# FFN2 of two batches as seven block products, four softmax products on another engine, and a new order of pieces

## The chip, the cores and the metric

The kernel runs on one core of a Trainium2 chip. The metric is the device time of one execution in microseconds, as the median of several runs. The core has five engines, each of which works through its own queue in order: TensorE (PE, matmuls into PSUM), VectorE (DVE), ScalarE (ACT), GpSimd (POOL) and SyncE (SP, which here only issues DMAs). PSUM is one tile of eight banks, each 128 partitions by 512 float32. DMAs are issued by POOL (loads that cast float32 to bfloat16, and phi), SP and ACT (stores).

## The reference

The input is q, k, v with 8 batches, 8 heads, 576 positions and 64 columns, phi with 32 memory slots, and four weights. Attention goes through the slots, and a feed-forward network with a maximum of three products follows:

```python
a = exp(phi - max_s(phi)); a = a / sum_s(a)                 # over the 576 positions
k_m = einsum('bhsm,bhsd->bhmd', a, k)                       # 32 slots a head
v_m = einsum('bhsm,bhsd->bhmd', a, v)
attn = softmax(q @ k_m^T / 8)                               # over the 32 slots
x = (attn @ v_m), heads side by side                        # 4608 rows, 512 columns
h = maximum(maximum(x @ w1, x @ w2), x @ w3)                # 768 columns
out = h @ w_out                                             # 4608 rows, 512 columns
```

## The kernel before, in words

The work is cut into pieces. The string of words at lines 594 to 617 is the order in which they are issued: a word like `F6@1!` is piece F with index 6 of batch 1, and the mark `!` swaps the engine that empties PSUM (`EVAC`, line 164, gives the usual one: a for ACT, v for DVE). Each engine gets its instructions in this order, so the order of words is the order within every engine and every queue. A second string (lines 138 to 146) says which PSUM bank each piece takes; a piece that takes a bank waits until the piece that had it before has been emptied. Nothing else schedules the work.

The pieces, by letter:

- L and H load: `L0@b` is phi, `L1@b` k, `L2@b` v, `L3@b` q of batch b (lines 85 to 112), all but the first phi issued by POOL. A load is put behind whatever POOL has been given before it. k and v have two buffers (`kvo`), so have phi and q. Y loads the weights.
- E (line 229) takes the exponential of phi on ACT. r (line 103) packs k (`r0`) or v (`r1`) on POOL into `kvr`, beside a column of ones.
- B (line 249) multiplies the exponentials with k, v and the ones: 72 small matmuls. N (lines 269 to 290) normalises on DVE, K (line 298) transposes the result on PE.
- Q (line 313) transposes q on DVE, in two halves. S (line 333) makes the scores of a batch from them on PE, and ACT takes two exponentials (line 342).
- a, s, c, m, X (lines 387 to 417) are the softmax over the 32 slots, per half g of the heads: DVE transposes in blocks of 32, sums, takes the reciprocal, POOL multiplies (m, line 409), DVE transposes back into `attn`.
- D (line 440) folds the values into the weights: `D0` to `D2` give `wp` for w1 - w3 and w2 - w3, `D3` gives `wp3` for the part of w3 that goes straight to the output (w3 times w_out, made once). Batch 0 has other columns.
- F (line 466) is the first layer: twelve per batch, four matmuls of 288 columns each. An even one is emptied through a relu into `h`, an odd one goes through a maximum on DVE with the `h` before it into `hT` (line 479).
- T (lines 497 and 506) is FFN2 for 128 rows: six matmuls of `hT` with w_out and two of `attn` with `wp3`, 512 columns each, then a copy to `ot` and a store of 256 KB by SP. Two batches have 1152 rows, nine tiles; `T4` is the tile that spans both. The last tile of all is done in two halves (lines 538 and 546).
- W, O, V prepare weights at the start; Z, I, M, R belong to the start as well.

The part of this order that the prediction follows is where batches 2 to 4 overlap (lines 601 to 607) and where B, S and the packs of each batch stand.

Of the kernel before, what the change touches and what calls it, by code (L numbers as in the profile page):

```python
# [8 lines left out]
FP32 = mybir.dt.float32  # L9
BF16 = mybir.dt.bfloat16  # L10
# [5 lines left out]
def kernel(  # L16
# [33 lines left out]
    opool = ctx.enter_context(tc.tile_pool(name="opool", bufs=6))  # L50
# [34 lines left out]
    def load_ph(b):  # L85
        ph = inp.tile([P, NP, NC, M], FP32, name="ph")
        loaded.setdefault(b, {})["ph"] = ph
        dst = ph.rearrange("p j c m -> p j (c m)")
        if b == 0:
            for h in halves:  # L90
                nc.sync.dma_start(out=dst[:, h], in_=by_pair(phi, b)[:, h])
        else:
            nc.gpsimd.dma_start(out=dst, in_=by_pair(phi, b))

    def load_kv(b, i, h=slice(0, NP)):
        kv = loaded.setdefault(b, {})["kv"] = kvos[b % 2]
        nc.gpsimd.dma_start(  # L97
            out=kv[:, 1 - i, h].rearrange("p j c d -> p j (c d)"),
            in_=by_pair((k, v)[i], b)[:, h],
        )  # L100

    def pack(b, i):
        nc.gpsimd.tensor_copy(  # L103
            out=kvrs[b % 2][:, :, :, D * i : D * (i + 1)], in_=kvos[b % 2][:, 1 - i]
        )
# [125 lines left out]
    def k_and_ones(kv, r, j, c):  # L231

        flat = kv[r].rearrange("p i j c d -> p (i j c d)")
        k0 = (NP * NC + j * NC + c) * D
        step = 2 * NP * NC * D - k0
        return flat[:, k0 : k0 + 2 * step].rearrange("p (i x) -> p i x", i=2)[:, :, 0:D]

    def att_kv(b, part=None):
        s = st[b]
        kvp = two_banks()  # L240
        s["kvp", part] = kvp
        kv = loaded[b]["kv"]
        nd = {None: 2 * D + 1, 0: 2 * D, 1: D}[part]
        kvr = kvrs[b % 2]
        for c in range(NC):
            for j in range(NP):
                for a in range(NG):
                    r = slice(HP * a, HP * (a + 1))
                    nc.tensor.matmul(  # L249
                        kvp[M * j : M * (j + 1), a, 0:nd],  # L250
                        lhsT=s["e"][r, j, c, :],
                        rhs={
                            None: lambda: kvr[r, j, c, 0:nd],
                            0: lambda: k_and_ones(kv, r, j, c),
                            1: lambda: kv[r, 0, j, c, :],
                        }[part](),
                        start=(c == 0),
                        stop=(c == NC - 1),
                        tile_position=(HP * a, M * j),
                    )  # L260

    def att_kv_norm(b, part=None):
# [16 lines left out]
        if part == 1:  # L279
            return  # L280
        for g in range(NG):
# [3 lines left out]
                in0=kvp[:, g, 0:D]  # L285
# [77 lines left out]
    def ones_rec(b, g):  # L363
# [7 lines left out]
        r = work.tile([P, S], FP32, name="r")  # L371
# [84 lines left out]
    def ffn1(b, n, swap):  # L456
# [20 lines left out]
        else:  # L477
# [6 lines left out]
            )  # L484

# [75 lines left out]
    def issue(b, n, swap):  # L561
# [8 lines left out]
            "r": lambda: pack(b, i),  # L570
# [9 lines left out]
            "m": lambda: att_mul(b, i),  # L580
# [5 lines left out]
            "T": lambda: ffn2(b, i, swap),  # L586
            "W": lambda: w3_t(i, swap),
# [6 lines left out]
    for w in """  # L594
        E@0 H2@0 H0@0 L3@0 Z25@0 B0@0 Y2@0 I@0 N0@0 Z2@0 K0@0! Q0@0 Q1@0 Z9@0 S@0 Z2@0 M0@0 M1@0
        R0@0 R1@0 W0@0 Y3@0 W1@0 W2@0 Z6@0 O1@0 H3@0 O3@0 O2@0 H1@0 X1@0 B1@0 X0@0 N1@0
        K1@0 O0@0 Y0@0 D1@0! D0@0! D3@0 F8@0 F10@0 F2@0 V0@0 F6@0 F0@0! Y1@0 D2@0 D4@0 F4@0
        L0@1 V1@0 F1@0 E@1 F3@0 L1@1 F5@0 F9@0 F7@0 L3@1 F11@0 B0@1 T3@0 N0@1 K0@1! L2@1 Q1@1
        L2@2 L1@2 Q0@1 L0@2 V2@0 T0@0! L3@2 S@1 T1@0 a0@1 s0@1 c0@1 m0@1 B1@1 N1@1 a1@1 L1@3
        K1@1 s1@1 D0@1 D1@1! D2@1 c1@1 m1@1 X0@1 L3@3 r1@2 X1@1 T2@0! L2@3 F6@1 F10@1 F7@1 F2@1  # L600
        F3@1 F4@1 F0@1 r0@2 E@2 F5@1 F1@1 F11@1 L0@3 L0@4 F8@1 L2@4 F9@1 B@2 D3@1 N@2 Q1@2
        T0@1! K@2 T2@1! r0@3 Q0@2 S@2 a0@2 a1@2 s1@2 c1@2 m1@2 T4@1! D1@2! s0@2 D2@2 c0@2 m0@2
        X1@2 D0@2 T3@1 Q0@3 L3@4 X0@2 Q1@3 T1@1 F0@2 F4@2 F8@2 F6@2 F9@2 E@3 F7@2 r1@3 F5@2
        F10@2 F1@2 B@3 L1@4 D3@2 N@3 L0@5 F2@2 F11@2 E@4 F3@2 L1@5 K@3 r1@4 L2@5 T2@2! S@3 T3@2
        a0@3 s0@3 c0@3 m0@3 D0@3 D2@3 a1@3 s1@3 c1@3 X0@3 D1@3! Q0@4 m1@3 T1@2 L3@5 L2@6 T0@2!
        X1@3 F10@3 r0@4 F2@3 F4@3 E@5 Q1@4 r0@5 F5@3 F3@3 L1@6 F8@3 B@4 N@4 D3@3 F9@3 F6@3
        F11@3 L0@6 K@4 F0@3 F7@3 F1@3 S@4 a0@4 T4@3! s0@4 a1@4 D0@4 c0@4 s1@4 r1@5 c1@4 D3@4
        m0@4 X0@4 Q0@5 T0@3! D1@4! D2@4 B@5 T3@3 m1@4 X1@4 L0@7 F10@4 Q1@5 N@5 F8@4 K@5 F6@4
        F9@4 S@5 F7@4 L3@6 F2@4 F4@4 a0@5 L1@7 a1@5 F0@4 s0@5 r1@6 F3@4 D0@5 r0@6 s1@5 c1@5 E@6
        D3@5 m1@5 c0@5 F1@4 T1@3 L2@7 F11@4 L3@7 E@7 F5@4 m0@5 B@6 D1@5! D2@5 X1@5 N@6 T2@3!  # L610
        X0@5 F6@5 F8@5 Q0@6 Q1@6 K@6 F4@5 F9@5 S@6 F7@5 r0@7 a0@6 F2@5 a1@6 s0@6 c0@6 F0@5
        F10@5 m0@6 F1@5 s1@6 c1@6 F11@5 F5@5 T0@4! F3@5 X0@6 T2@4! r1@7 D0@6 D1@6! Q0@7 B@7
        m1@6 N@7 X1@6 T2@5! K@7 T3@4 Q1@7 S@7 a0@7 F2@6 s0@7 a1@7 s1@7 c1@7 m1@7 c0@7 F4@6
        T4@5! D3@6 D2@7 D0@7! T0@5! D3@7 D2@6 X1@7 m0@7 D1@7! T1@4 X0@7 F6@7 F3@6 T1@5 F4@7
        F8@7 F0@7 F5@6 F10@6 F7@7 F9@7 F10@7 F5@7 F0@6 F11@7 F6@6 F1@7 F7@6 F2@7 F8@6 F11@6
        F9@6 F1@6 F3@7 T0@6! T0@7! T3@5 T2@7! T2@6! T1@6 T1@7 T3@6 T4@7! T3@7
    """.split():
        n, b = w.rstrip("!").split("@")
        issue(int(b), n, w.endswith("!"))
# [30 lines left out]
```

## Time and profile before

| what | us |
|---|---|
| median of 3 runs | 164.94 |
| lowest, highest | 164.56, 165.78 |
| span of the profiled execution, first to last instruction | 163.3 |
| PE busy | 153.8 |
| ACT, DVE, POOL busy | 100.6, 90.4, 69.5 |

The profiled execution comes with its span and not with a time of its own; the median of the runs is 1.6 us above that span. The mean granted clock of TensorE was 0.995. The page gives for each group of instructions the line, engine, operation, tile, shapes, count, the busy time with the mean of one, and the idle time before it with what ended it. The chain follows the last instruction back to what released it, step by step. The DMA share of a window is the mean busy share of the 16 DMA engines; it can go above 1 where packets of two queues overlap.

### The profile page before, as it was taken

The page shows a single profiled execution, that of the slowest core. Times are in us where ns is not written, and L with a number is a line of the kernel's source. Part 1 is how long each engine was busy: PE and PEld are TensorE (multiplying, and loading weights), DVE is VectorE, ACT ScalarE, POOL GpSimd, SP SyncE. Part 2 cuts the span into 40 slices and gives each one's busy share as a digit, 9 for nine tenths or more (in the row PEclk, how much of TensorE's full clock was granted, in tenths as well). Part 3 has the DMA queues.
Part 4 walks back from the last instruction along what each step waited for, and adds up shares of the span by engine and source line. Part 5 has one row for each costly group of instructions (what it writes and reads, how often), then busy time and mean ns, then how long its engine had stood idle before and what let it go on. Part 6 is the DMA issues. An engine that isn't in the chain of part 4 may idle for free.

```text
span 163.3 us, 4838 instructions
## 1 busy us (share of the span) xinstructions
PE 153.8 (94%) x2080; PEld 85.3 (52%) x2080; DVE 90.4 (55%) x181; ACT 100.6 (62%) x151; POOL 69.5 (43%) x71
## 2 busy tenths in 40 slices
PE   7978798899899999999999999999999999999990
PEld 2433444564377436743673575576553468744450
DVE  2023704798838665849399748879749128810010
ACT  4205445845497488778885899994658976223320
POOL 7932205100599259657968957646403100000000
PEclk9999999999999999999999999999999999999998
DMA  6999999999999999999999999996313130014333
GB/s 150 152 206 207 205 210 217 274 208 210 253 313 238 209 253 379 274 210 293 252 263 206 232 355 264 191 233 150 130 69 129 69 128 0 0 68 186 135 128 130
DMA packets 21974, 31.77 MB, mean 195 GB/s; under 512 B 1216, under 2 KB 16576, under 8 KB 21952
## 3 DMA queue, kind: packets, MB, share of 16 engines
q0 software_dynamic: 16080, 21.43, 68.7%
q1 hardware_dynamic: 5728, 9.90, 17.2%
q8 instruction: 16, 0.26, 0.6%
q10 hardware_dynamic: 144, 0.13, 0.2%
q14 instruction: 6, 0.05, 0.1%
HBM read 39.32 MB, written 9.44 MB: 299 GB/s over the span
## 4 chain that ended last, share of the span: by engine, by line
PE 83%; DMA 9%; POOL 2%; ACT 2%; issue 1%; DVE 1%; ACTq 0%; POOLq 0%
PE psum L497 29%; PE psum L466 28%; DMA wo_sb<-in_moe_w_out_dram 9%; PE psum L506 8%; PE psum L440 6%; PE psum L249 4%; PE psum L192 3%; PE psum L333 2%; PE psum L515 1%; ACT h L170 1%; PE psum L538 1%; PE psum L298 1%; POOL kvo L97 1%; ACT wp L172 1%; POOL qq L110 0%
## 5 line engine op out<-in xcount | busy, mean ns | idle before, releaser
L497 PE MATMUL psum<-wo_sb,hT 128*128 128x512 bf16 x210 | 51.3, 380 | 0.0
L466 PE MATMUL psum<-attn,wp 128*128 128x288 bf16 x384 | 50.5, 286 | 0.1
L479 DVE TENSOR_TENSOR hT<-psum,h 128x576 bf16<-128x576 f32 x48 | 34.2, 749 | 18.0 <-PE psum L466 12.5
L466 PEld LDWEIGHTS <-wp 128*128 128x128 bf16 x384 | 36.7, 98 | 13.2 <-issue 2.0
L172 ACT COPY ot<-psum 128x512 f32<-128x512 f32 x35 | 20.7, 591 | 32.1 <-PE psum L506 25.2
L497 PEld LDWEIGHTS <-hT 128*128 128x128 bf16 x210 | 19.2, 97 | 24.0 <-issue 4.3
L172 ACT CAST wp<-psum 128x1024 bf16<-128x1024 f32 (+1 forms) x31 | 29.2, 995 | 3.8 <-PE psum L440 2.0
L103 POOL COPY kvr<-kvo 128x2304 bf16<-128x2304 bf16 x12 | 25.3, 2111 | 13.7 <-DMA kvo<-in_k_dram 10.1
L170 ACT ACTIVATE h<-psum 128x576 bf16<-128x576 f32 x47 | 28.4, 659 | 3.5 <-PE psum L466 3.3
L409 POOL TENSOR_TENSOR t<-t,sm 128x576 bf16<-128x576 bf16 x14 | 16.1, 1154 | 24.6 <-DVE sm L404 24.4
L506 PE MATMUL psum<-wp,attn 128*128 128x512 bf16 x62 | 18.4, 379 | 0.0
L159 PE MATMUL psum<-warm 128*128 128x512 bf16 x44 | 12.1, 427 | 1.2 <-DVE warm L128 1.2
L313 DVE STREAM_TRANSPOSE qT<-qq 128x576 f32<-128x576 f32 x16 | 11.7, 747 | 1.4 <-DMA qq<-in_q_dram 1.4
L342 ACT ACTIVATE e<-psum 128x576 bf16<-128x576 f32 x16 | 9.6, 652 | 3.8 <-PE psum L333 3.8
L229 ACT ACTIVATE e<-ph 128x1152 bf16<-128x1152 f32 (+1 forms) x9 | 9.6, 1065 | 1.7 <-DMA ph<-in_phi_dram 1.6
L395 DVE TENSOR_REDUCE sm<-t 128x18 f32<-128x576 bf16 x14 | 10.3, 738 | 0.2
L387 DVE STREAM_TRANSPOSE t<-e 128x288 f32<-128x288 f32 x14 | 6.4, 465 | 6.2 <-ACT e L342 6.1
L97 POOL DMA_DIRECT2D kvo<-in_v_dram x9 | 6.7, 749 | 7.1 <-PE psum L249 4.1
L506 PEld LDWEIGHTS <-attn 128*128 128x128 bf16 x62 | 6.1, 98 | 7.1
L110 POOL DMA_DIRECT2D qq<-in_q_dram x8 | 6.2, 770 | 6.6 <-DVE h L174 3.7
L555 DVE COPY ot<-psum 128x256 f32<-128x256 f32 x1 | 0.4, 425 | 15.4 <-PE psum L546 15.4
L249 PEld LDWEIGHTS <-e 64*32 64x32 bf16 x720 | 6.9, 90 | 3.7 <-issue 3.3
(57 smaller groups left out, 114.4 us busy)
## 6 DMA issues: line engine op xcount, KB each, us to landing
out_dram<-ot SPq DMA_DIRECT2D x35, 256.0 KB, 5.6
qq<-in_q_dram POOLq DMA_DIRECT2D x8, 576.0 KB, 12.2
ph<-in_phi_dram POOLq DMA_DIRECT2D x7, 576.0 KB, 14.4
kvo<-in_k_dram POOLq DMA_DIRECT2D x7, 576.0 KB, 14.6
kvo<-in_v_dram POOLq DMA_DIRECT2D x7, 576.0 KB, 15.6
w_sb<-in_moe_w_dram POOLq DMA_DIRECT2D x3, 768.0 KB, 19.0
wo_sb<-in_moe_w_out_dram POOLq DMA_DIRECT2D x1, 768.0 KB, 14.6
ph<-in_phi_dram SPq DMA_DIRECT2D x2, 288.0 KB, 3.0
```

The source lines that it names most:

```text
L103: nc.gpsimd.tensor_copy(out=kvrs[b % 2][:, :, :, D * i : D * (i + 1)], in_=kvos[b % 2][:, 1 - i])
L159: nc.tensor.matmul(po[:, 0:BANK], lhsT=warm[:, 0:P], rhs=warm, start=True, stop=True)
L170: nc.scalar.activation(out=out_, in_=in_, func=AF.Relu)
L172: nc.scalar.copy(out=out_, in_=in_)
L249: nc.tensor.matmul(kvp[M * j : M * (j + 1), a, 0:nd], lhsT=s["e"][r, j, c, :], rhs={None: lambda: kvr[r, j, c, 0:nd], 0: lambda: k_and_one ...
L313: nc.vector.transpose(out=s["qT"][:, j].rearrange("p j c r e -> p (j c r e)").bitcast(FP32), in_=loaded[b]["q"][:, j].rearrange("p j c d - ...
L395: nc.vector.tensor_reduce(out=sm, in_=s["t", g].rearrange("p n r e -> p n e r"), op=ALU.add, axis=mybir.AxisListType.X,)
L409: nc.gpsimd.tensor_tensor(out=t, in0=t, in1=s["sm", g].unsqueeze(2).to_broadcast([P, S // HP, R, 2]), op=ALU.mult,)
L466: nc.tensor.matmul(acc[:, h, 0:SH], lhsT=wps[b][:, g, w * DF + ft * P : w * DF + (ft + 1) * P], rhs=attn[:, g, c0 : c0 + SH], start=(g == ...
L479: nc.vector.tensor_tensor(out=hT[:, ft, (b % 2) * S : (b % 2 + 1) * S].rearrange("p (h n) -> p h n", h=2), in0=a, in1=s["h1", ft], op=ALU.max,
L497: nc.tensor.matmul(po, lhsT=hT[:, fc, c0 : c0 + P], rhs=wo_sb[:, fc, :], start=(n == 0), stop=False,)
L506: nc.tensor.matmul(po, lhsT=attn[:, g, c0 : c0 + P], rhs=wp3s[b][:, g, :], start=False, stop=(g == NG - 1),)
```

## The change

Three things change.

First, tiles T0 to T3 of batches 5 and 6 (512 rows each) are replaced. The 512 rows, the inner dimension (768 columns of `hT` and 256 of `attn`) and the 512 output columns are halved, and the product is made of seven block products (Strassen in Winograd's form): four sums of blocks of the left side (pieces A: `A0` to `A3` on `hT`, 768 elements a partition, `A4` to `A7` on `attn`, 256 elements), four of the right side (pieces U: on w_out once, as `U@9`, and on each batch's `wp3`), seven products of eight matmuls with 256 columns (pieces P), copies of partial sums out of PSUM, and sums on DVE that write the output blocks. Two stores of 512 KB each take the place of four of 256 KB. Sums run on POOL or DVE as the mark says. `A2` is written over its own input in `hT`.

Second, four of the softmax products m (`m1@1`, `m0@2`, `m1@2`, `m1@3`) carry the mark and run on DVE.

Third, the order string and the bank string are new. Marks move other work as well: K of batches 2 to 5 and 7 is emptied by ACT, and some of T, D and F by DVE. The order of loads changes, and with it POOL's queue. `kvo` has its ones ahead of k and v, so that one access pattern reads ones and k; the pool of output tiles has four buffers instead of six.

```diff
-    opool = ctx.enter_context(tc.tile_pool(name="opool", bufs=6))
+    opool = ctx.enter_context(tc.tile_pool(name="opool", bufs=4))
...
+    KV = NP * NC * D
+    ones_k = [const.tile([P, D + 2 * KV], BF16, name=f"kvo{i}") for i in range(2)]
...
-    def att_mul(b, g):
+    def att_mul(b, g, swap):
...
-        nc.gpsimd.tensor_tensor(
+        (nc.vector if swap else nc.gpsimd).tensor_tensor(
             out=t,
...
+    KT = FT // 2
+    CH = DM // 2
+    TW = 2 * P
...
+    tw = w3T.rearrange("p f j n -> p (f j n)").rearrange("p (i k c) -> p i k c", i=4, k=KT)
+    sa0 = const.tile([P, 4, TW], BF16, name="sa0")
+    oj0 = [const.tile([P, 2, DM], FP32, name=f"oj{i}") for i in range(2)]
+    SNAP = {0: "m5", 1: "m1", 4: "u2"}
...
+    def combine(on_dve, out_, in0, in1, op):
+        eng = nc.vector if on_dve else nc.gpsimd
+        eng.tensor_tensor(out=out_, in0=in0, in1=in1, op=op)
+
+    def combine_w(b, i, on_dve):
...
+        in0, in1 = [(x[B12], x[B11]), (x[B22], t[0]), (x[B22], x[B12]), (x[B21], t[1])][i]
+        combine(on_dve, t[i], in0, in1, SUB)
...
+    def combine_a(b, i, on_dve):
+
+        s, sa = sums(b)
+        n = i % 4
+        if i < 4:
+            (a11, a12), (a21, a22) = blocks(hts[b // 2], b, KT)
+            t = {0: s[:, 0], 1: s[:, 1], 2: a21, 3: s[:, 2]}
+        else:
+            (a11, a12), (a21, a22) = blocks(attns[b // 2], b, 1)
+            t = {m: sa[:, m : m + 1] for m in range(4)}
+        in0, in1 = [(a21, a22), (t[0], a11), (a11, a21), (a12, t[1])][n]
+        combine(on_dve, t[n], in0, in1, ADD if n == 0 else SUB)
+
+    def products(b, i, swap):
...
+        lhs, rhs, name = [
+            (summed(0), w_summed(0), "y"),
+            (plain(0, 0), w_plain(0, 0), "x"),
+            (plain(0, 1), w_plain(1, 0), "z"),
+            (summed(3), w_plain(1, 1), "y"),
+            (summed(1), w_summed(1), "x"),
+            (summed(2), w_summed(2), "x"),
+            (plain(1, 1), w_summed(3), "x"),
+        ][i]
...
+        for k in range(KT + 1):
+            for q in range(2):
+                nc.tensor.matmul(
+                    po[:, q * CH : (q + 1) * CH],
+                    lhsT=lhs(k, q),
+                    rhs=rhs(k),
+                    start=(i < 3 and k == 0 and q == 0),
+                    stop=(k == KT and q == 1),
+                    skip_group_check=True,
+                )
...
+        if i in SNAP:
+            t = ln if i == 0 else work.tile([P, S], FP32, name="snap", tag="r")
+            t = acc[SNAP[i]] = t[:, 0:DM].rearrange("p (q n) -> p q n", q=2)
+            copy(t, x)
...
+        if i == 6:
+            copy(ot, x)
+        else:
+            if i == 4:
+                x = acc["y"].rearrange("p (q n) -> p q n", q=2)
+            y = acc[{2: "m1", 4: "u2", 5: "m5"}[i]]
+            nc.vector.tensor_tensor(out=ot, in0=x, in1=y, op=ADD)
+        if i in (4, 6):
...
+            nc.sync.dma_start(out=rows[:, :, i // 5], in_=acc["ot"][i // 5])
...
-            "m": lambda: att_mul(b, i),
+            "m": lambda: att_mul(b, i, swap),
...
+            "U": lambda: combine_w(b, i, swap),
+            "A": lambda: combine_a(b, i, not swap),
+            "P": lambda: products(b, i, swap),
```

The new order from the start of batch 3's loads to the scores of batch 4, and from the scores of batch 7 to the end:

```
F9@1 L0@3 B@2 N@2 Q1@2 D3@1 T0@1 K@2! Q0@2 T2@1 S@2 L1@3 E@3 a0@2 s0@2 c0@2
T4@1! a1@2 s1@2 D3@2 D0@2 L3@3 D2@2 m0@2! c1@2 X0@2 L2@4 T3@1 T1@1 m1@2! D1@2!
X1@2 L1@4 r1@3 L0@4 r0@3 Q1@3 B@3 F6@2 N@3 F7@2 F2@2 F0@2 Q0@3 F3@2 K@3! F10@2
F1@2 S@3 F11@2 F4@2 F8@2 L2@5 r1@4 E@4 a1@3 a0@3 F5@2 F9@2 D1@3! D3@3 L3@4 T0@2!
U1@9! s1@3 r0@4 c1@3 D0@3 B@4 D2@3 L1@5 L0@5 s0@3 L3@5 T2@2! N@4 K@4! c0@3 T3@2
Q0@4 r1@5 L0@6 m0@3 Q1@4 S@4 m1@3! T1@2 ...
... S@7 a0@7 T4@5! A1@5!
a1@7 X0@6 D3@7 s1@7 X1@6 D1@6! c1@7 s0@7 D0@7! P0@5 P1@5 c0@7 P2@5 A2@5 A3@5!
F4@6 P3@5! m0@7 F5@6 X0@7 F0@6 P4@5! F8@6 F2@6 F6@6 U0@6! U3@5 P5@5! m1@7 D2@7
D1@7! F1@6 P6@5 X1@7 F9@6 F7@6 F0@7 U1@6 F6@7 F3@6 F10@6 A4@6! F2@7 F11@6 F1@7
A6@6! A0@6 F4@7 F8@7 A1@6! F10@7 A5@6! F3@7 F9@7 A2@6! P0@6 A7@6! F5@7 U3@6 F7@7
F11@7 P1@6! U2@6! A3@6 P2@6 T2@7! P3@6! P4@6 T1@7 P5@6 T0@7 P6@6 T4@7! T3@7
```

In it B@7 stands ahead of all twelve F of batch 5, and `r1@7`, the pack of v of batch 7, stands on POOL between `m1@5` and `m0@5`. The banks of this stretch are, for D1@3 and D0@3, 0 and 1; for D3@3 and D2@3, 4 and 5; for T3@2, 4.

## The prediction

> **What bounds the kernel now.** First the page: TensorE (PE) is busy for 94% of the span, and the chain that ended last is PE for 83%. Then the chain in order of time, whose columns are start, length, what:
>
> ```profile
> 35.84 1.40 PE psum L497 x6
> ...
> 46.13 5.88 PE psum L466 x48
> ...
> 85.95 0.41 PE psum L333 x23
> ...
> 116.63 0.65 PE psum L249 x69
> ...
> 142.07 1.29 PE psum L497 x6
> 143.37 0.43 PE psum L506 x2
> ...
> 158.71 0.66 PE psum L538 x6
> ```
>
> L333 at 85.95 is the score piece of batch 4 (S@4), L249 at 116.63 the key-value piece of batch 7 (B@7). From 31 us on it is matmul after matmul. A piece F (four matmuls of 288 columns) costs 5.88/12 = 0.49 us, a tile of T 1.29 + 0.43 = 1.72, a matmul of 256 columns 0.66/6 = 0.11. Six matmuls cost 1.40 after the small-tile forms (B, S, D) and 1.29 otherwise: 0.11 for such a step. Then I asked what stands next to PE. The table by windows gives us, busy time of PE, PEld, DVE, ACT, POOL, granted clock, DMA share, GB/s:
>
> ```profile
> 60.00:80.00 20.00, 20.00 (x246) 11.37 (x245) 13.46 (x28) 16.65 (x25) 14.70 (x14) 1.00 1.14 288
> 80.00:110.00 30.00, 29.98 (x550) 18.14 (x548) 23.08 (x50) 26.27 (x39) 21.03 (x17) 1.00 1.17 248
> 110.00:115.00 5.00, 5.00 (x34) 3.13 (x32) 4.93 (x10) 2.04 (x4) 3.73 (x4) 1.00 0.63 136
> ```
>
> The DMA engines are as full as PE until about 112 us (a share over 1: packets overlap). GpSimd's (POOL's) timeline shows that consumers live at the edge of this stream:
>
> ```profile
> 51.19 1.50 POOL L93 DMA_DIRECT2D ph<-in_phi_dram  x2
> 52.67 0.77 POOL L97 DMA_DIRECT2D kvo<-in_v_dram  x1
> 56.34 2.11 POOL L103 COPY kvr<-kvo 128x2304 bf16<-128x2304 bf16 x1 [2.90 <-DMA kvo<-in_k_dram]
> ...
> 71.38 2.11 POOL L103 COPY kvr<-kvo 128x2304 bf16<-128x2304 bf16 x1 [2.30 <-DMA kvo<-in_v_dram]
> ...
> 108.46 2.10 POOL L103 COPY kvr<-kvo 128x2304 bf16<-128x2304 bf16 x1 [3.58 <-DMA kvo<-in_k_dram]
> ```
>
> A pack starts the moment its k or v lands. So there are two bounds: PE work, and a load queue that lands in order of issue. A new order that asks for data earlier must find them landed.
>
> **The DMA pace, from rows.** In the DMA issues by window, q1 is issued at 16.11 and lands 21.6 us later, v1 at 19.92 and 20.6 later: 2.84 us apart, with no store between. A phi load adds 1.56 (k2 lands at 48.47, phi2 at 50.03). Between q2 (31.21 + 22.3 = 53.5) and v7 (102.15 + 9.65 = 111.8) land 14 full loads, 5 phi and 14 stores in 58.3 us; 14 x 2.84 + 5 x 1.56 = 47.6, so a store of 256 KB adds 0.77.
>
> **Removed and added on PE.** Eight tiles of T go: 8 x 1.72 = 13.8. Fourteen products of 8 matmuls with 256 columns come: 112 x 0.11 = 12.3. The order has 23 steps from small-tile forms instead of 25: -0.2. Sum -1.7 us, all on the path. The weight load of each matmul (L538's PEld row: 98 ns) stays just below the 110 ns pace; were it exposed at 130 ns, 112 x 0.02 = 2.2 us would come back.
>
> **Moved: batches 3 and 4.** S@4 started at 85.95. Ahead of it the new order no longer has the twelve F@3 (5.88) and T1@2 (1.72), so PE wants it at 78.3. What it needs:
>
> - phi4. Before, its issue at 51.93 stood ahead of v4 (landed 67.2). Now L0@4 is behind the pack of v3 on POOL, so behind k3, q3, v4 and k4. It lands 5 full loads, 2 phi and the 5 stores of T@1 after q2: 53.5 + 14.2 + 3.1 + 3.9 = 74.7. E@4 (1.17, L229) waits for it on ACT, in order, until 75.9; behind it stand the evacuations D1@3, D3@3 (1.02 each), T0@2 (0.59), D0@3, D2@3: 76.9, 77.9, 78.5, 79.5, 80.6. D0@3's matmuls reuse banks 0-1 of D1@3, so PE waits from about 74 to 76.9. T3@2 reuses bank 4 of D2@3: from 80.6, and S@4 follows at 82.3.
> - q4. Now behind phi4 and v5: 74.7 + 2 x 2.84 + 0.77 = 81.1, plus both transposes on DVE (2 x 0.74, L313): 82.6 for S@4's second half.
>
> Both ways say 82.5 where PE wants 78.3: **+4.2 us**. Queued behind Q1@4 on DVE are m1@3, X0@3, a0@4 and X1@3 (0.75 + 3 x 0.47, to 84.8); F8@3 needs the last, and PE reaches it after S@4 and T1@2 at 84.6: 0.2 more at most. The earlier waits (q3 lands at about 65.3, k4 at 73) are inside it.
>
> **Moved: batch 7.** The twelve F@5 leave the place ahead of B@7 (5.9 us; two T and two D change places with others): it is wanted at 116.63 - 5.9 = 110.7, with the wait above 114.9. The set of loads up to v7 is the same, so it lands at 111.8, or 110.5 with up to two stores fewer served; pack 2.11, so 112.6 to 113.9: covered, but only by the 4.2. Behind that pack POOL holds m0@5, whose result F6@5 needs 2.7 us after B@7 starts; 1.15 + 0.47 fits.
>
> **Costed at nothing.** The elementwise work grows by row sums about 20 us on DVE (to 111) and 13 on POOL (to 82), and shrinks by 7 on ACT: all below PE's 154.
>
> - Sums on POOL (U, A): L409 gives 1.15 us per 576, so 1.54 for 768 and 0.51 for 256; the other end is L103's one-input 0.92 ns per element (0.7), and twice L409 (3.1) as a bound for the strided reads. I take 1.54, the nearest in kind. On DVE: L213's 684 ns for 1024 gives 0.56 for 768; L377's 1.3 ns per element gives 1.0.
> - The tight chain is batch 6. Between F11@6 and P0@6 PE has six F (2.94); DVE has two max (0.75 each) and A0 (0.56), with 0.2 for the hand-over 2.26: cover 0.7. P3@6 needs A1 (POOL), then A3 (DVE); PE has P0, P1, P2, three F and T2@7 between (5.8), and A3 ends some 0.8 before. At POOL's dear end A1, A5, A2 and A7 take 8.2 and A7 comes late for P3: 1 us. Batch 5 has 1.9 us of cover, and loses 1.2 at the dear end.
> - The four softmax products on DVE: 0.75 (L377) in place of 1.15 on POOL; between L213's rate (0.39) and 1.15 I take 0.75.
> - Snapshots and sums of PSUM: 0.59 (L172) on ACT, 0.68 on DVE (L479 for 512). P5@5's sum must end before P6@5 writes its bank: D2@7, D1@7 and F1@6 stand between (1.05), 0.68 and the hand-over leave 0.2 us of cover; T tiles or several F stand between elsewhere.
> - opool with 4 tiles: T1@1 reuses T0@1's, whose store landed at 61.2; its copy is due after 64. Otherwise the copy waits.
> - The 512 KB stores: the last has T4@7 and T3@7 (3.6 us) before the final ones; 256 KB alone took 2.0, 128 KB 1.7, so an estimate of 2.6.
>
> **Sum.** 163.3 - 1.7 + 4.2 = 165.8 us of span. The profiled execution gives the span alone, and the median of the runs (164.94) lies 1.6 us above it, so **167.4 us**. A measurement of this kernel tells a change of over 1% (1.65 us) from none.
>
> **A rule against it.** PE's longest wait here after 31 us is 0.4 us, and the granted clock was 1.00 in the three stretches shown; the new wait before D0@3 is 2.7 to 3.5 us. The first 25 warm-up matmuls took 7.28 us where 25 x 0.216 = 5.4 would do: a cold start costs 1.9. The Trainium skill ("TensorE: Matmul & The Clock Gate", section "HAM oscillation — how this bites in real kernels") asks for no PE-idle gap over about 3.4 us, lest the clock halve; no run here shows that in mid-kernel. By it, the sum stays if the gap is shorter, and is 169.3 if it is longer.
>
> **Rivals.**
>
> - Only batch 7 is held (chance 0.22): phi4 and q4 land some 3 us sooner than I reckon, and B@7 waits for v7 alone: 113.7 - 110.7 - 1.7 = +1.3, 166.2. For it: my landings add up seven and nine loads. Against: eight of the twelve packs of L103 begin on a landing.
> - The other side, nothing waits (0.07): if the load queue had slack of 4 us or more from batch 3 on, PE stays full and the 1.7 us are gained, 163.2. It decides where phi4 lands before 71. Against: DMA share 1.14 to 1.17.
> - A cold start (0.05): the wait before D0@3 lasts long enough to cost the 1.9 us of the warm-up: 169.3.
> - More is lost (0.11): POOL's sums at the dear end (1 to 2), exposed weight loads (2.2), or DVE, held behind q3 and q4, handing its lateness on: 168.5 to 170.
> - The forecast (0.55): 167.4, itself good to 1 us.
>
> The range leaves out the second rival and the far ends: 165.3 to 169.8. Slower by over 1%: 0.68; within 1%: 0.28; faster by over 1%: 0.04.
>
> **What would show it.** Right: ACT idle before one `e<-ph` activation until a landing near 75 us; qT's transposes for batch 4 after a landing near 81; PE idle of 2.5 to 3.5 us before a fold (D) near 74 and some 4 us in all before 83; products at 0.11 us a matmul with no gap after 115. Wrong: PE full between 60 and 83, or waits on POOL's sums near the end.

## The result, and the profile after

The changed kernel takes 167.06 us (median of 8 runs, 166.31 to 167.67); the kernel before, run beside it, takes 165.14 (8 runs, 164.56 to 166.45). The ratio is 1.0111 with a 95% interval of 1.0078 to 1.0144: slower, by just over 1%; the interval excludes equal times, but reaches below the 1% that the forecast called tellable. The forecast was 167.4, with a range of 165.3 to 169.8. The profiled execution has a span of 164.6 us, where the forecast's sum was 165.8 and the kernel before had 163.3; that execution took 166.58 us, 2.0 above its span.

The busy times and the chain come first, as the page of the changed kernel has them (engine, busy us, share of the span, instructions; then the chain's shares by engine):

```profile
PE 151.5 (92%) x2109; PEld 90.8 (55%) x2128; DVE 111.8 (68%) x208; ACT 94.6 (57%) x142; POOL 85.0 (52%) x87
...
PE 54%; DMA 29%; POOL 8%; issue 4%; ACT 1%; DVE 1%; ACTq 0%; POOLq 0%
```

PE's share of the chain fell from 83% to 54%, and DMA has 29%: the chain now runs through the load queue, as forecast. The windows that were shown of before (PE, PEld, DVE, ACT, POOL busy, granted clock, DMA share, GB/s) look like this now:

```profile
60.00:80.00 20.00, 19.58 (x366) 10.98 (x339) 16.08 (x34) 18.02 (x26) 12.40 (x10) 1.00 1.17 250
80.00:110.00 30.00, 29.37 (x449) 17.57 (x453) 24.74 (x47) 21.07 (x32) 20.68 (x18) 1.00 1.16 264
110.00:115.00 5.00, 4.84 (x126) 2.26 (x126) 3.67 (x8) 4.81 (x7) 4.19 (x3) 1.00 0.60 184
```

Here the surprise begins. The forecast wanted 2.5 to 3.5 us of idle PE before D0@3 and some 4 us in all before 83, and named PE full between 60 and 83 as a sign of being wrong. PE lacks only 0.42 us in the first of these windows, and what it lacks after 50 us is mostly gaps of 0.16 us in front of tiles that show five matmuls in place of six: matmuls that the profile did not record (it has 2109, that of the run e1_m_pool below 2128). The list of PE's waits (engine, line, what was waited for: total us, times, longest) says where the time went:

```profile
PE psum L468 <- DVE attn L419: 2.4, 1, 2.4
...
PE psum L250 <- DMA kvo<-in_k_dram: 0.8, 1, 0.8
PE psum L300 <- DVE kvn L274: 0.4, 1, 0.4
PE psum L300 <- DVE kvn L285: 0.4, 1, 0.4
PE psum L250 <- DMA kvo<-in_v_dram: 0.4, 1, 0.4
```

Apart from the gaps of missing records (L657, behind the dots, 1.1 in all), all of it lies ahead of 50 us. L468 is F (L466 before) and L419 the transpose X that writes `attn`: F0@1 waited 2.44 us, at 46.7 to 49.1, for the softmax of batch 1. DVE's timeline (start, length, engine, line, operation) shows why, and POOL's beside it:

```profile
44.66 0.27 DVE L406 RECIPROCAL sm<-sm 128x18 f32<-128x18 f32 x1
44.96 3.64 DVE L411 TENSOR_TENSOR t<-t,sm 128x576 bf16<-128x576 bf16 x1
48.52 0.82 DVE L419 STREAM_TRANSPOSE attn<-t 128x288 f32<-128x288 f32 x2
```

```profile
44.34 0.79 POOL L113 DMA_DIRECT2D qq<-in_q_dram  x1
45.12 0.75 POOL L98 DMA_DIRECT2D kvo<-in_v_dram  x1
45.85 2.13 POOL L108 COPY kvr<-kvo 128x2304 bf16<-128x2304 bf16 x1
48.30 2.27 POOL L108 COPY kvr<-kvo 128x2304 bf16<-128x2304 bf16 x1 [0.32 <-DMA kvo<-in_v_dram]
```

L411 is m1@1, one of the four softmax products that moved to DVE. It took 3.64 us. The other three took 0.75, 0.71 and 0.72, as forecast. Beside the long one POOL had a pack.

And yet the forecast's own chain is there, up to D0@3 almost to the tenth. The chain in order of time (start, length, what) and PE's timeline:

```profile
58.80 15.82 DMA ph<-in_phi_dram
75.71 1.00 ACT wp L175
```

```profile
76.76 0.41 PE L442 MATMUL psum<-w_sb,kvt 64*32 64x512 bf16 x8
...
81.80 0.49 PE L335 MATMUL psum<-qT,kvt 32*32 32x288 bf16 x32
```

phi4 lands at 58.80 + 15.82 = 74.62 (forecast 74.7), its exponential ends and D1@3 is evacuated by 76.71, D0@3 starts at 76.76 (76.9), S@4 at 81.80 (82.5). Only that PE, late by 3.6 us from its waits before 50 us (2.44 for the product, 0.81 and 0.35 for k and v of batch 1), got to D0@3 at that very moment and did not have to wait.

So two readings fit one profile. **Theory A:** two bounds lie side by side, the stretched product and the load queue, and each alone holds PE at D0@3 until 76.7; to remove one gains little. **Theory L:** the stretched product alone made the loss, and the loads came just in time.

### The profile page after: what moved, and what is told of

Its sections match the earlier page's. It is cut to its first block, busy times and chain, and to the rows that moved or that the text cites. A ratio compares the mean times of both kernels' runs of the same rounds, so it can differ in the third digit from the quotient of the medians.

```text
span 164.6 us, 4936 instructions
## 1 busy us (share of the span) xinstructions
PE 151.5 (92%) x2109; PEld 90.8 (55%) x2128; DVE 111.8 (68%) x208; ACT 94.6 (57%) x142; POOL 85.0 (52%) x87
## 4 chain that ended last, share of the span: by engine, by line
PE 54%; DMA 29%; POOL 8%; issue 4%; ACT 1%; DVE 1%; ACTq 0%; POOLq 0%
PE psum L468 18%; PE psum L657 15%; DMA kvo<-in_k_dram 14%; DMA ph<-in_phi_dram 10%; PE psum L600 7%; DMA qq<-in_q_dram 6%; PE psum L666 4%; POOL kvr L108 4%; PE psum L442 3%; POOL kvo L98 3%; PE psum L250 2%; PE psum L335 1%; PE psum L675 1%; POOL qq L113 1%; PE psum L698 1%
## 5 line engine op out<-in xcount | busy, mean ns | idle before, releaser
L468 PE MATMUL psum<-attn,wp 128*128 128x288 bf16 x384 | 50.1, 286 | 2.5 <-DVE attn L419 2.4
L468 PEld LDWEIGHTS <-wp 128*128 128x128 bf16 x384 | 36.9, 98 | 14.2 <-issue 3.9
L657 PE MATMUL psum<-wo_sb,hT 128*128 128x512 bf16 x146 | 37.0, 380 | 1.6 <-issue 1.1
L173 ACT ACTIVATE h<-psum 128x576 bf16<-128x576 f32 x44 | 26.9, 653 | 11.3 <-PE psum L468 10.9
L175 ACT CAST wp<-psum 128x1024 bf16<-128x1024 f32 (+1 forms) x28 | 26.6, 991 | 3.0 <-PE psum L442 3.0
L175 ACT COPY ot<-psum 128x512 f32<-128x512 f32 x21 | 12.4, 589 | 20.5 <-PE psum L666 14.2
L657 PEld LDWEIGHTS <-hT 128*128 128x128 bf16 x162 | 14.4, 98 | 17.5 <-issue 4.2
L411 POOL TENSOR_TENSOR t<-t,sm 128x576 bf16<-128x576 bf16 x10 | 11.5, 1156 | 21.4 <-DVE sm L406 21.4
L666 PE MATMUL psum<-wp,attn 128*128 128x512 bf16 x46 | 13.7, 379 | 0.0
L442 PE MATMUL psum<-w_sb,kvt 64*32 64x512 bf16 (+1 forms) x200 | 8.8, 373 | 0.6 <-DVE kvt L179 0.3
L250 PEld LDWEIGHTS <-e 64*32 64x32 bf16 x720 | 7.1, 90 | 3.7 <-issue 2.7
L98 POOL DMA_DIRECT2D kvo<-in_k_dram x9 | 6.9, 767 | 3.8 <-DMA qq<-in_q_dram 2.1
L162 PEld LDWEIGHTS <-warm 128*128 128x128 bf16 x44 | 4.6, 113 | 7.6 <-issue 3.9
```

The source lines that it names most:

```text
L98: nc.gpsimd.dma_start(out=kv[:, i, h].rearrange("p j c d -> p j (c d)"), in_=by_pair((k, v)[i], b)[:, h],)
L162: nc.tensor.matmul(po[:, 0:BANK], lhsT=warm[:, 0:P], rhs=warm, start=True, stop=True)
L173: nc.scalar.activation(out=out_, in_=in_, func=AF.Relu)
L175: nc.scalar.copy(out=out_, in_=in_)
L442: nc.tensor.matmul(ps[M * j : M * (j + 1), a, 0 : hi - lo], lhsT=lhs[r, M * j : M * (j + 1)], rhs=rhs[r, j, :], start=(i == 0), stop=(i == ...
L468: nc.tensor.matmul(acc[:, h, 0:SH], lhsT=wps[b][:, g, w * DF + ft * P : w * DF + (ft + 1) * P], rhs=attn[:, g, c0 : c0 + SH], start=(g == ...
```

## The experiments

Medians are in us; each ratio is to runs of the kernel before on the same chip, taken between those of the kernel. The fourth column is the sum of PE's waits of more than 0.1 us after 31 us in the profiled execution, without the gaps that are missing records; the next is where the last matmul ends.

| kernel | median (runs) | ratio to before, 95% | PE waits | PE ends | span |
|---|---|---|---|---|---|
| before | 165.14 (8) | | 0.75 | 159.58 | 163.3 |
| changed | 167.06 (8) | 1.0111 (1.0078 to 1.0144) | 3.92 | 161.19 | 164.6 |
| e1_m_pool | 166.65 (10) | 1.0094 (1.0064 to 1.0123) | 3.20 | 161.17 | 164.6 |
| e6_pack_later | 167.12 (4) | 1.0139 (1.0066 to 1.0211) | 3.64 | 161.53 | 165.0 |
| e2_loads | 169.22 (4) | 1.0249 (1.0194 to 1.0305) | 4.28 | 163.91 | 167.4 |
| e3_both | 167.38 (4) | 1.0144 (1.0066 to 1.0222) | 3.30 | 164.08 | 167.5 |
| e7_phi4 | 168.53 (4) | 1.0219 (1.0155 to 1.0284) | 4.58 | 162.16 | 165.6 |
| e8_order | 167.61 (4) | 1.0149 (1.0114 to 1.0184) | 3.16 | 162.12 | 165.6 |
| e9_k3 | 167.65 (4) | 1.0155 (1.0124 to 1.0186) | 3.36 | 162.31 | 165.8 |
| e5_tiles | 170.70 (4) | 1.0344 (1.0307 to 1.0381) | 4.51 | 164.45 | 168.2 |
| e10_splice | 164.63 (10) | 0.9963 (0.9950 to 0.9976) | 2.29 | 159.74 | 163.2 |
| e11_splice | 163.51 (6) | 0.9906 (0.9869 to 0.9942) | 0.98 | 158.82 | 162.3 |
| e12_m_dve | 177.56 (4) | 1.0749 (1.0688 to 1.0810) | 8.83 | 171.57 | 175.3 |

All edits but the last are in the order string (and banks) of the changed kernel or the kernel before.

### One product back on POOL

```diff
-s1@1 c1@1 L0@2 m1@1! D0@1 m0@1 X0@1
+s1@1 c1@1 L0@2 m0@1 m1@1 D0@1 X0@1
```

> The changed kernel with one of its four softmax products, m1@1, back on POOL behind m0@1; nothing else differs. In the changed kernel that product took 3.64 us on DVE where its three sisters took 0.71 to 0.75, a pack of POOL ran beside it, and PE waited 2.44 us for its result before F0@1. Theory A (two bounds side by side): PE would have waited for phi4 and q4 in any case, so the 2.44 us saved at 47 us are lost again before D0@3 and S@4; E@4 ends at about 75.8, D0@3 starts at 76.7, S@4 at 81.9, span 164.2 to 164.6, a gain of 0 to 0.4. Theory L (the stretched product alone made the loss): F0@1 starts at 46.7, everything behind it 2.4 us earlier, span 162.2.

Measured: 166.65 us, span 164.6, PE's last matmul at 161.17 where the changed kernel had 161.19. The 2.44 us are gone and nothing is gained in the span. The median is 0.4 us lower; the last section has a likely reason. PE's waits in this run:

```profile
PE psum L442 <- ACT wp L175: 1.7, 1, 1.7
...
PE psum L250 <- POOL kvr L108: 0.7, 1, 0.7
...
PE psum L468 <- DVE kvn L285: 0.3, 1, 0.3
```

L442 is D0@3: it waits 1.72 us for the evacuation of D1@3, which stands on ACT behind the exponential of phi4, and it starts at 76.76 as in the changed kernel. L250 is B@3, held by the pack of k3; the last is F behind q3. S@4 starts at 81.81. Theory L falls, and the half of theory A that concerns the load queue is shown: it holds PE at D0@3 until 76.7 by itself. For the other half there is the timing of the changed kernel, and of e5_tiles below, where F0@1 waited 2.54 and D0@3 then only 0.43, to start at 76.68.

### The pack somewhere else

```diff
-L2@3 r0@2 F7@1 F8@1 E@2 r1@2 F1@1
+L2@3 r1@2 F7@1 F8@1 E@2 r0@2 F1@1
```

> The changed kernel with the two packs of batch 2 exchanged on POOL: the pack of v2 (which waits for its landing at about 48.2 us) stands ahead of the pack of k2. m1@1 stays on DVE, now with the two DMA issues of POOL beside it and no pack. If the pack of POOL stretches the product: m1@1 takes 0.7 to 0.8 us and F0@1 starts at about 46.7. If the DMA issues or something else in the DVE queue stretch it: it takes 1.5 us or more again and F0@1 starts at 47.5 to 49. In the span, theory A gives 164.2 to 164.6 and theory L 162.2, as with the product on POOL.

```profile
44.02 0.76 DVE L411 TENSOR_TENSOR t<-t,sm 128x576 bf16<-128x576 bf16 x1
```

```profile
43.62 0.79 POOL L113 DMA_DIRECT2D qq<-in_q_dram  x1
44.40 0.75 POOL L98 DMA_DIRECT2D kvo<-in_v_dram  x1
47.39 2.10 POOL L108 COPY kvr<-kvo 128x2304 bf16<-128x2304 bf16 x1 [2.25 <-DMA kvo<-in_v_dram]
```

With the same two DMA issues beside it but no pack ready to run, m1@1 takes 0.76 us. The pack is what stretched it. The span is 165.0, because D0@3 waits 1.70 again and B@3 waits 1.43 for its pack: theory A once more.

### The loads earlier, and each wait replaced by the next

```diff
-X0@2 L2@4 T3@1 ... L1@4 r1@3 L0@4 r0@3 ... D3@3 L3@4 T0@2!
+X0@2 L0@4 L2@4 T3@1 ... L1@4 r1@3 L3@4 r0@3 ... D3@3 T0@2!
-D0@3 B@4 D2@3 ... T2@2! N@4 K@4! c0@3 T3@2 Q0@4 r1@5 L0@6 m0@3 Q1@4 S@4 m1@3! T1@2 ... F8@3
+D0@3 D2@3 ... c0@3 L3@5 m0@3 T2@2! B@4 T3@2 N@4 m1@3! K@4! r1@5 L0@6 X0@3 X1@3 T1@2 Q0@4 Q1@4 S@4 ... F8@3
```

This is e2_loads; e3_both has the edit of e1_m_pool as well.

> The changed kernel with its loads in another order only: phi4 is issued ahead of v4, q4 right behind the pack of v3, and B@4 and S@4 stand a little later among the pieces of batches 2 and 3 so that PE has other work until k4 and q4 land. m1@1 is still on DVE. Landings should move to about 70 us for phi4 and 77 for q4. Theory A and theory L agree here: PE arrives 2.4 us late from the stretched product, and the loads were just hidden behind that, so 0 to 0.4 us is gained: span 164.2 to 164.7. If the load queue had been the only loss, and the stretched product harmless, it would be 162.2 or less.

> Both edits of the two runs before this one together: m1@1 on POOL and phi4 and q4 earlier. Theory A: now neither bound holds PE, F8@3 is reached at about 81.6 in place of 84.1, and then B@7 becomes the next wait, because the pack of v7 cannot end before about 112.7; span 163.2 to 163.6, a gain of 1.0 to 1.4, more than the two edits gave singly. Theory L: the same 162.2 that m1@1 alone gives, and no more than that run.

The landings came within 2 us of what was expected (e3: phi4 68.26, q4 77.98 in place of 74.62 and 80.12 in e1_m_pool), the times did not: spans 167.4 and 167.5, and for e3_both a median of 167.38. The new order gained nothing. In both, F8@3 stands right behind S@4 and waits 1.3 us for the banks that ACT empties of the scores; T1@2, which covers that in the changed kernel, had been moved ahead of S@4. PE's timeline of e3_both:

```profile
83.43 0.47 PE L335 MATMUL psum<-qT,kvt 32*32 32x288 bf16 x24 [0.34 <-DVE qT L315]
85.19 1.05 PE L468 MATMUL psum<-attn,wp 128*128 128x288 bf16 x4 [1.29 <-ACT e L344]
```

The four matmuls of the second line take 1.05 us where a piece F takes 0.65 in this view: PE had come back at half its granted clock. The windows of the same execution (PE busy, granted clock, DMA share, GB/s):

```profile
85.00:86.00 1.00, 0.81 (x4) 0.65 1.06 304
86.00:87.00 1.00, 1.00 (x7) 0.50 1.11 290
87.00:88.00 1.00, 1.00 (x6) 0.50 1.14 275
88.00:89.00 1.00, 1.00 (x7) 0.65 1.16 255
```

Fourteen matmuls come every 0.24 us in place of 0.12, a loss of 1.6. The profiled execution is the slowest of the four; the others have spans of 165.1, 164.9 and 165.9 at a clock of 1.00, no better than e1_m_pool (164.3 to 165.2 but for one). In e2_loads m1@1 took 3.85 us, F0@1 waited 2.65, and PE came back at half its clock there too. So these two runs say little on the sum of the two edits; e3_both shows that the wait before D0@3 goes away with an earlier phi4. The smaller edit, e7_phi4 (the edit of e1_m_pool and only phi4 earlier), tells more:

> m1@1 on POOL as in the run e1_m_pool, and one thing more: the load of phi4 is issued ahead of v4 and k4 instead of behind them; q4 and the order of the pieces stay. In e1_m_pool PE waited 1.72 us before D0@3 for phi4's exponential. Theory A: phi4 lands at about 68, the wait before D0@3 goes, but k4 now lands at about 74.8 and its pack ends near 77, so B@4, which stands right behind D0@3, waits until 77 instead; then S@4 waits for q4, which still lands at about 80, until 81.6. The span is 164.2 to 164.6 again: each wait is replaced by the next thing in the load queue. If phi4 alone were the cause, all 1.72 us would come back: span 162.9.

```profile
PE psum L250 <- POOL kvr L108: 2.1, 2, 1.3
...
PE psum L335 <- DVE qT L315: 0.9, 2, 0.6
```

D0@3 waits no longer; B@4 behind it waits 1.27 for the pack of k4 until 76.79, then S@4 waits 0.60 and 0.34 for q4. Each wait was replaced by the next in the load queue, as theory A said. The span is 165.6, 1 us above what was expected, and all of that is S@4: its first matmuls start 0.34 us later than in e1_m_pool, and most of them wait once more for the second half of q4. So T1@2 behind it starts 0.99 us later, and PE ends 0.99 later. The first two lines are of e7_phi4, the third is of e1_m_pool:

```profile
82.81 0.46 PE L335 MATMUL psum<-qT,kvt 32*32 32x288 bf16 x24 [0.34 <-DVE qT L315]
83.20 1.47 PE L657 MATMUL psum<-wo_sb,hT 128*128 128x512 bf16 x6
...
82.21 1.47 PE L657 MATMUL psum<-wo_sb,hT 128*128 128x512 bf16 x6
```

The runs spread (167.47 to 169.75); the profiled one is the fastest of them, and why the others are slower is open.

### A whole new order, and k3 first

e8_order moves U@9, the softmax products of batch 3, B@4, S@4, some F@3, and B@7, so that PE has other work while loads land. m1@3 goes back to POOL with them. e9_k3 also lands k3 ahead of phi3. The core of it:

```diff
-D1@3! D3@3 L3@4 T0@2! U1@9! s1@3 r0@4 c1@3 D0@3 B@4 D2@3 ... T2@2! N@4 K@4! c0@3 T3@2 ... S@4 m1@3! T1@2
+D1@3! D3@3 T0@2! s1@3 c1@3 m1@3 D0@3 s0@3 c0@3 m0@3 D2@3 r0@4 X1@3 T2@2! X0@3 ... F8@3 Q0@4 F4@3 T3@2 Q1@4 F9@3 B@4 ... K@4! F0@3 S@4 T1@2
```

> m1@1 on POOL, phi4 and q4 issued earlier, and an order that no longer asks for data early: U1@9 moves to a place where DVE is idle, the softmax products of batch 3 stand ahead of the pack of k4, so that F@3 can fill PE while k4 and q4 land; B@4 and S@4 stand behind some F@3; B@7 stands behind F6@5 and m0@5 ahead of the pack of v7. The work is the same. Theory A (the early loss is nothing but demands ahead of the load queue): of the 2.7 us of waits that e1_m_pool still had, 1.7 go; the 0.7 before B@3 and 0.3 behind it stay, and nothing new comes up to the end; span 162.7 to 163.2, about the kernel before. If PE is held by something that moves along (DVE, a bank), F8@3 or S@4 will show a new gap of over 1 us and the span stays above 164.

> As e8_order, with the loads of batch 3 exchanged: k3 is issued ahead of phi3, and the exponential of phi3 stands later on ACT. In e1_m_pool B@3 waited 0.70 us for the pack of k3, and F waited 0.28 us behind q3. k3 should land at about 60 and phi3 at 61.8; B@3 then starts at about 63.5 without a wait, all that follows comes 0.7 earlier unless q3 (landing near 65.9) holds it again. Theory A: span 162.0 to 162.5, the first of these that is faster than the kernel before (163.3). If q3 or v7 takes over, 162.7 to 163.2 as in e8_order.

Both missed: spans 165.6 and 165.8, medians 167.61 and 167.65. Of the old waits of batch 3 the one behind q3 is left (0.53, in e9_k3 1.08) and 0.19 before S@3, but new ones came: 0.53 and 0.36 on DVE's maxima near 89 to 90, 0.33 near 114, and in e8_order 0.76 at B@2. Waits sum to 3.16 and 3.36, as much as in e1_m_pool, and PE ends 1 us later. PE's timelines show where. From the start of D0@3 to the start of B@5 all three runs hold the same pieces: e1_m_pool takes 15.55 us for them (76.76 to 92.31), e8_order 17.45 (74.98 to 92.43), e9_k3 17.44. So the 1.8 us by which D0@3 came earlier in e8_order are lost again: 0.89 in the two waits for the maxima, and 1.0 in steps of 0.07 to 0.3 us at the changes between pieces (S@4 holds PE for 0.60 us until the next piece, where it was 0.41), which no list of waits counts. The rest comes around B@7: at K@7 behind it e8_order is 0.83 us late, 0.33 of it the wait near 114. Why the changes between pieces cost more in this order is open. In e8_order m1@2, on DVE, met a pack again: 2.56 us.

### The products undone

e5_tiles has the changed kernel's order with tiles T0 to T3 of batches 5 and 6 as before, and no sums of blocks.

```diff
-P0@5 P1@5 c0@7 P2@5 A2@5 A3@5! F4@6 P3@5! m0@7 F5@6 X0@7 F0@6 P4@5! ... P6@5
+T0@5! T1@5 c0@7 T2@5! F4@6 m0@7 F5@6 X0@7 F0@6 T3@5 ...
-P0@6 A7@6! F5@7 U3@6 F7@7 F11@7 P1@6! U2@6! A3@6 P2@6 T2@7! P3@6! P4@6 T1@7 P5@6 T0@7 P6@6 T4@7! T3@7
+T0@6! F5@7 F7@7 F11@7 T1@6 T2@6! T2@7! T3@6 T1@7 T0@7 T4@7! T3@7
```

> The changed kernel's order with tiles T0 to T3 of batches 5 and 6 computed as plain tiles again (six matmuls of 512 columns and two more each) at the places of the products; no sums of blocks, no snapshots, stores of 256 KB. Everything up to 115 us is the same, so the losses of the early part stay. The forecast's step says that the products save 13.8 - 12.3 = 1.5 us of PE on the path: this run should have PE full from 115 us on and end 1.4 to 1.6 us later than the changed kernel, span about 166.1. If sums or stores cost the products something that no gap shows, the difference is smaller; at the end where weight loads are exposed it would be nothing.

170.70 us, 3.6 above the changed kernel, where 1.5 was expected. The last stretch is clean in both kernels: from the first tile or product of batch 6 to the last matmul, 147.03 to 164.44 here and 144.56 to 161.19 there, 17.41 against 16.63: 0.78 for batch 6, which is the expected size (seven products at 0.87 for four tiles at 1.72). The rest, some 1.8, arose between 132 and 141 us, where four waits of 0.13 to 0.34 stand, for evacuations, and the pieces behind them run longer. That belongs to the places where I put the tiles, and is no gain of the products.

### The products without the early order

e10_splice takes the order of the kernel before up to S@6, and the changed kernel's from S@7 on.

```diff
 ... S@6 F7@5
+U0@9 U2@9
 r0@7 ... F3@5 X0@6 T2@4! r1@7 D0@6 D1@6! Q0@7 B@7
-m1@6 N@7 X1@6 T2@5! K@7 T3@4 Q1@7 S@7 a0@7 F2@6 ... T0@5! ... T1@5 ... T3@7
+D3@6 m1@6 A4@5! N@7 X1@6 A5@5! A7@5! T1@4 U0@5! K@7 T3@4 Q1@7 U2@5 U1@5 A6@5! S@7 U1@9! U3@9
+A0@5 a0@7 T4@5! A1@5! ... P0@5 P1@5 ... P6@6 T4@7! T3@7
```

> The products of the change without its early order: the order and banks of the kernel before, word for word, up to the scores of batch 6 (so all softmax products before that on POOL, phi4 and q4 ahead of what follows, all twelve F@3 before S@4 and the twelve F@5 before B@7), then T1@4 in place of T2@5 to cover the normalisation of batch 7, and the changed kernel's order for the rest, with the seven products for T0 to T3 of batches 5 and 6. U@9 and the sums on attn go on POOL and DVE while r0@7 waits for k7 and behind the pack of v7. The work is that of the changed kernel. If the changed kernel's loss is only its early order, as theory A says, PE is full from 31 us on as before, and the step of the products, 1.5 to 1.7 us, shows in the end: span 161.6 to 162.0 against 163.3 before, median 163.3 to 163.8, ratio 0.990 to 0.993. If the products or their sums cost PE something that the early loss covered, new gaps of 0.5 us or more come up after 115 us and the ratio is 0.997 or more.

164.63 us, ratio 0.9963 (0.9950 to 0.9976): 0.4% faster than the kernel before, less than expected. Up to B@7 PE waits little more than before and comes to it 0.6 us later; then it waits once, 1.08 us, before T1@4, whose bank ACT had yet to empty of D1@6. That was my choice of bank. e11_splice mends it:

```diff
-B@7[2] D3@6[6] m1@6 ... T1@4[4] U0@5! K@7[0] T3@4[5] Q1@7
+B@7[2] m1@6 ... T1@4[6] K@7[7] T3@4[5] D3@6[6] U0@5! Q1@7
```

> As e10_splice, with one bank and one place mended. There PE waited 1.08 us before T1@4, because T1@4 took the bank of D1@6, whose evacuation on ACT was still under way. Now T1@4 takes bank 6 (emptied long before), K@7 bank 7, and D3@6 stands behind T3@4. Theory A: the 1.08 us goes, nothing takes its place, PE ends near 158.7 and the span of the runs is 161.6 to 161.9 where the kernel before has 163.0 to 163.6: median 163.5 to 163.8, ratio about 0.990. If ACT or the sums hold the next piece instead, the ratio stays at 0.996.

163.51 us, ratio 0.9906 (0.9869 to 0.9942), the interval of a gain of 0.6 to 1.3%. This version beats both kernels, though the gain is at the edge of the 1% that the forecast called tellable. In medians it is 1.7 us; the profiled execution, the second slowest of six, has a span 1.0 us shorter than that of the kernel before, and from B@7 to the last matmul PE takes 41.8 us (117.05 to 158.82) where it took 43.1 (116.45 to 159.58). The group of F shows how little PE waits (line, operation, busy us and mean ns, idle before):

```profile
L468 PE MATMUL psum<-attn,wp 128*128 128x288 bf16 x384 | 51.1, 286 | 0.3 <-issue 0.2
```

So the change held two things: products that are worth about what the forecast said, and a part ahead of them, the early order with its four products on DVE, that cost more than they gave.

### The four softmax products alone

e12_m_dve is the kernel before with one part of the change.

```diff
-        nc.gpsimd.tensor_tensor(
+        (nc.vector if swap else nc.gpsimd).tensor_tensor(
...
-c1@1 m1@1 X0@1 ... c1@2 m1@2 ... c0@2 m0@2 ... Q0@4 m1@3 T1@2
+c1@1 m1@1! X0@1 ... c1@2 m1@2! ... c0@2 m0@2! ... Q0@4 m1@3! T1@2
```

> The kernel before with one part of the change alone: m1@1, m0@2, m1@2 and m1@3 on DVE; order, banks, loads and tiles stay. If a pack of POOL that is ready to run stops a softmax product on DVE: m1@1 starts at about 44.4 with the pack of v2 next on POOL, ends some 0.6 us after that pack, 2 to 3.5 us in place of 0.75, and F6@1 starts 1 to 2 us later than the 46.13 of the kernel before; the other three, with no pack beside them, take 0.7 to 0.75 us. The span is then 164.2 to 165.3. If the stretch belongs to the changed kernel's order alone, all four take 0.75 us and the span is 163.0 to 163.5.

177.56 us, 12 us slower: the direction was right, the size far off. m1@1 took 3.42 us beside its pack; m0@2 and m1@2 took 0.76; and m1@3 this:

```profile
82.28 6.48 DVE L409 TENSOR_TENSOR t<-t,sm 128x576 bf16<-128x576 bf16 x1
82.67 4.17 POOL L103 COPY kvr<-kvo 128x2304 bf16<-128x2304 bf16 x2
...
86.77 0.74 POOL L97 DMA_DIRECT2D kvo<-in_k_dram  x1
87.50 0.76 POOL L93 DMA_DIRECT2D ph<-in_phi_dram  x1
88.25 2.48 POOL L103 COPY kvr<-kvo 128x2304 bf16<-128x2304 bf16 x1
88.80 0.48 DVE L417 STREAM_TRANSPOSE attn<-t 128x288 f32<-128x288 f32 x1
...
89.33 0.88 PE L466 MATMUL psum<-attn,wp 128*128 128x288 bf16 x3 [5.34 <-DVE attn L417]
```

Two packs stood back to back, and a third behind two DMA issues; the product ended only as the third ran. PE waited 2.12, 0.62 and 5.34 us for `attn`, 8.1 in all. Twice it came back at half its granted clock (0.50 in the windows of 1 us from 49 to 51 and from 88 to 92), which at some 1.6 to 1.7 us each makes most of what is left of the 12 us.

## Why the prediction was right, and where it was not

**The time and the sign were right, the way there in half its parts, and that the time came within 0.4 us is luck.** In the profiled execution one loss was missed and the other overrated, and the sum for the span was 1.2 us too large (165.8, measured 164.6). The median came out close to 167.4 all the same, because it lies 2.5 us above that span, where the forecast took 1.6. By the steps of the forecast:

- **Products, -1.7 on PE.** Right. A product takes 0.87 us, a tile 1.72; e5_tiles shows 0.78 for batch 6. Without their waits after 31 us PE has 159.58 - 31 - 0.75 = 127.8 us of work before and 161.19 - 31 - 3.92 = 126.3 after: 1.5 to 1.6 less. e11_splice turns it into 1.7 us of time. Exposed weight loads, which would have brought 2.2 back, did not show; no run has the 130 ns of that term, a weight load of the products took 98 ns.
- **Landings.** Right within 1 us: phi4 74.62 (74.7), k4 72.90 (73), q3 64.52 (65.3), q4 80.14 (81.1), v7 110.63 (110.5 to 111.8). The pace from rows, 2.84 us for a load, 1.56 for phi and 0.77 for a store, in order of issue, is what can be carried on.
- **The stall, +4.2 in batches 3 and 4.** The mechanism was right and its size too large. e1_m_pool, where nothing else delays PE, has the chain as it was told, and it costs 0.70 at B@3, 0.28 at F and 1.72 at D0@3: 2.7. In front of S@4 one error is q4, which landed 1 us sooner; the other is where PE would be without the stall, 81.81 - 2.7 = 79.1 at S@4 and not 78.3. In the changed kernel itself this wait was not seen, for PE came to it late already; PE was full between 60 and 83, which the forecast had named as a sign of being wrong.
- **Four softmax products at 0.75.** This step failed. The bounds were 0.39 and 1.15; one of the four took 3.64. I took the duration from a row of the same shape on DVE (L377), whose neighbours on POOL I did not look at, and priced the move by what it adds to DVE's busy time. What the move costs is a wait for a copy on POOL: 2.4 us on PE, which here fell into the same hole as the load queue's 2.7. The time came out near the forecast because the two losses did not add up, and the load queue's had been overrated by 1.5.
- **Sums on POOL and DVE at nothing.** Right: POOL 1.65 for 768 elements and 0.67 for 256 (1.54 and 0.51 were taken), DVE 0.55 (0.56; `A2@5` 0.78), and no wait for any of them between 115 us and the end, where PE is busy for 44.84 of 45 us.
- **Batch 7.** Right that it was covered: the pack of v7 ended at 113.07 and B@7 started at 113.75. Without the 2.7 us lost earlier PE would by this sum have come at some 111 and waited, so the cover is the loss, as the forecast said; no run shows that wait. It never became the bound, in e11_splice either, where the order of before leaves twelve F@5 ahead of it.
- **The rivals.** "Only batch 7 is held" and "nothing waits" fell, and of "more is lost" neither POOL's dear end nor exposed weight loads showed. The cold start, given 0.05, was given to the wrong wait, but it is real; that is the last section.

What the experiments leave open: why the changes between pieces cost 1 us more in e8_order and e9_k3, and so whether an order with the early demands could be saved at all.

## What to carry to other kernels

A transfer of work between engines is priced by what its new engine will run beside, not by its busy time: in these runs a VectorE operation with both inputs in SBUF took up to 6.5 us in place of 0.75 where GpSimd had copies ready to run. When two waits can hide each other, remove both before judging either, and ask of a queue that is full what is next in it: e1_m_pool and e7_phi4 each removed a true wait and gained nothing in the span. And when a change joins a good part with an order that costs, splice: the old order up to the last point where the new part needs nothing, the new one from there (e11_splice, 0.9906).

## What was not expected of the hardware

**DVE stands still while POOL copies.** Every DVE operation that took well over its usual time has two SBUF inputs, and POOL had an operation from SBUF to SBUF beside it, in the long cases a pack. m1@1 ended 0.6 us after the pack in the changed kernel (47.98, 48.60) and in e12_m_dve (47.05, 47.68); a sum of blocks, U1@9, took 2.17 in e1_m_pool where it takes 0.55 alone:

```profile
73.61 2.17 DVE L505 TENSOR_TENSOR w3T<-wo_sb,w3T 128x768 bf16<-128x768 bf16 x1
```

The pack there ran from 73.24 to 75.36. The maxima of F, which read PSUM and one input from SBUF, take 0.69 to 0.76 in all runs. The Trainium skill ("SBUF — State Buffer", section "Who interferes with whom") says just this: a VectorE instruction with two SBUF inputs contends with a GpSimd instruction that reads SBUF, and the one that issues first holds the shared ports for its whole length. The trace agrees on the block. On the order it agrees where the pack started first (U1@9 above; m1@2 of e8_order, which started 0.16 us after a pack and ended 0.61 after it), and once the other way: in e1_m_pool m1@2 started 0.33 us ahead of a pack that had just got its data and took 0.71, and the pack took 2.36 in place of 2.11. But m1@1 in the changed kernel started at 44.96, and the pack, by the profile, at 45.85, behind two DMA issues; 0.75 us would have been enough, and it lost all the same. In e6_pack_later, where the pack still waited for its data, it did not. That a pack which is ready counts as issued while POOL still shows the DMA issues ahead of it would explain both, and the 6.48 us too; it was not tested by itself, and it rests on the profile's start marks.

**Half the clock after idle PE.** Windows of 1 us of e2_loads (PE busy, granted clock, DMA share, GB/s), behind the 2.65 us for which F0@1 waited:

```profile
46.00:47.00 1.00, 0.00 (x0) 1.00 1.13 374
47.00:48.00 1.00, 0.00 (x0) 1.00 1.03 361
48.00:49.00 1.00, 0.44 (x3) 0.93 1.11 261
49.00:50.00 1.00, 1.00 (x6) 0.50 1.22 221
50.00:51.00 1.00, 1.00 (x6) 0.50 1.14 281
51.00:52.00 1.00, 1.00 (x6) 0.50 1.18 242
52.00:53.00 1.00, 1.00 (x9) 0.86 1.20 207
```

For about 3.4 us PE runs at half its clock, a matmul of F every 0.24 us where it takes 0.12, a loss of some 1.7 us. It happened after 2.12 us in e12_m_dve too, and in e3_both after 1.29 us that followed 0.34 us of idle PE and a score piece of 0.5 us. In the profiled run of the changed kernel it did not, after 2.44 us; but of its eight runs six have a mean granted clock of 0.987 to 0.990 and spans of 165.0 to 165.8, and two 0.998 and 1.000 and spans of 164.6 and 164.4. The six lie 0.8 us above the two. That this is the half clock behind F0@1 is likely but not shown, for these executions have no trace; nor is it shown why it is 0.8 and not 1.7. If so, the median of the changed kernel holds some 0.8 us that its profile does not show. In e1_m_pool, whose longest wait is 1.72 us, one run of ten has 0.990, and a span of 166.5 where the others have 164.3 to 165.2. The Trainium skill ("TensorE: Matmul & The Clock Gate", section "HAM oscillation — how this bites in real kernels") asks for no idle gap of over about 3.4 us. The measurements are stricter: 2.1 us were enough here in one run, 2.44 were not in another, and in e3_both it came after two short gaps of 1.6 us in all.
